# Sparse attention with two gated blocks on one core: PSUM as one pool of eight banks, two sets of scores at once, ScalarE subtracting half of the maxima, and the first y sums of both halves abreast

## The chip, the cores and the metric

The kernel runs on 1 core of one Trainium2 chip. The metric is device time in microseconds (us), the median of the runs of a kernel. The core has a matrix engine (TensorE, PE in the rows; its weight loads are PEld), a vector engine (VectorE, DVE), an activation engine (ScalarE, ACT), a general engine (GpSimd, POOL) and an engine that here only issues DMAs (SyncE, SP). Each engine executes its own instructions in the order in which they were written. Products are summed in PSUM, which has 8 banks of 512 fp32 columns over 128 partitions.

## The reference, cut to what matters

Three blocks follow each other, for a batch of 2, 768 positions, 8 heads of 64, and a width of 512:

```python
# attention: a window of 32 positions, and 24 summaries of 32 positions each
k_sum = k.reshape(B, H, nb, block, D).max(axis=3)
v_sum = v.reshape(B, H, nb, block, D).mean(axis=3)
scores_l = scale * np.matmul(q, k.transpose(0, 1, 3, 2))      # where |i-j| < 16
scores_s = scale * np.einsum('bhsd,bhnd->bhsn', q, k_sum) + np.log(block)
a = softmax(concatenate([scores_l_m, scores_s]));  x = a @ concatenate([v, v_sum])
# first block
theta = x @ w_theta
zr, zi = x * np.cos(theta), x * np.sin(theta)
y = np.einsum('ts,bsd->btd', w_tok_r, zr) + np.einsum('ts,bsd->btd', w_tok_i, zi)
u = x + y;  x = u + np.maximum(u @ w_ch, 0.0)
# second block
h = gelu(x @ w_in);  u, v = split(h);  v_n = layernorm(v) * g_ln
out = x + (u * (w_sg @ v_n + b_sg)) @ w_out
```

## The kernel before, in words

Every large product is made of three matmuls (`mm3`, L647 to L652: high by high, high by low, low by high), since each fp32 operand is split into a high and a low part by a copy and a subtraction.

The attention is cut into 8 pairs of heads (4 of each batch) and each pair into 2 halves of the sequence: 16 units, named by pair and half (`0_1` is pair 0, second half). A unit is a chain (`at_unit`, L871):

- `S`: PE lays masks (L881) and adds the scores (L890) in two PSUM banks, 3 tiles of 120 columns for each of 2 heads. That is one set of scores.
- `m`: DVE takes the 6 maxima (L923). `d`: DVE subtracts them (L929, 128x720) and writes `P` in SBUF; the set of scores is then free.
- `e`: ACT takes the exponential of `P` in place (L937, one instruction of 720 columns).
- `PT`, `Pt`: PE transposes `P` (L942, two groups of 3), ACT or DVE copies the result out of PSUM (L637, L642).
- `O`, `n`: PE multiplies by the values (L957, 24 matmuls), DVE divides by the sums (L967 to L971) and writes `x`.
- `X`, `xe`: PE transposes `x` (L980), ACT or DVE copies it to `xT`.

`ks` and `vs` are the summaries of k and v (L829, L837); `vp`, `vm`, `vr` lay the latter out with the values. Then `th` (L650 to L652 under `theta`) is x by w_theta, four groups of three matmuls of 512 columns for each of 12 tiles of 128 positions; `kk`, `rr`, `ab`, `sc`, `zm`, `zh`, `zl` turn it into sines and cosines times x, split into parts (`rotated`, L1036). `mixed` (L1072) sums y over the 6 tiles of a batch: 4 blocks of 6 matmuls (three of 512 columns into `y`, three of 256 into `ys`) for each tile and each half of the columns. A half of the columns needs 2 banks for `y` and 1 for `ys`. `uv` adds the result to `xT`. After that come `ch`, `iv`, `iu` (the products with w_ch and w_in), the layer norm, `Qp` (the product with w_sg, written to `Qs`) and `o` (the product with w_out, stored from SBUF).

The order of the work is made when the program is written. Each step is entered with `op` (L391): its engine or engines with an estimated duration, what it comes after, the buffers it takes and gives back, and a key. `Order.play` (L442) runs through these estimates and always takes the ready step with the smallest key. The keys come from three tables of numbers, `PLAN`, `LEAD` and `SHIFT`. Buffers have kinds: before, six single PSUM banks are of kind B and one pair of banks is of kind S, so that one set of scores exists at a time. Where the estimate has PE idle between 6 and 36 us, the planner puts in matmuls that nothing reads (`fill`, L707).

Of the kernel before, what the change touches and what calls it, by code (L numbers as in the profile page):

```python
# [8 lines left out]
F32 = mybir.dt.float32  # L9
# [6 lines left out]
ALU = mybir.AluOpType  # L16
# [21 lines left out]
    q_from=121.281, q_step=28.693, q_back=223.53, at0=-10.9, at0_pair=7.346, at0_half=2.395,  # L38
    at1=30.092, at1_pair=3.285, at1_half=4.867, th0=27.719, th0_step=4.256, th1=34.789,
    th1_gap=17.348, th1_step=24.005, y00=98.094, y00_step=24.656, y01=63.431, y01_step=19.591,  # L40
    y10=147.759, y10_step=8.224, y11=160.878, y11_step=12.492, k_early=56.892, vt_early=1.56,
    q_early=4.908, v_early=-11.766, s_early=11.963, pt=-73.034, o=3.795, x=51.425, y_gap=3,
    w_spare=2, v_spare=1, z_spare=6, y_spare=0, q_spare=2, table=13.626, mode=5.473, bsg=250.456,
    far0=6, far1=8, trees=109)
# [4 lines left out]
    Qz=74.168, ks=-40.136, vs=-11.881, vm=11.936, vr=-13.929, e=17.901, Pt=48.07, n=-10.669,  # L49
    xe=4.677, xh=9.148, xl=4.343, kk=-1.1, rr=-29.76, sc=-13.602, zm=-9.187, zh=7.556, zl=38.914,  # L50
    w_tht=8.728, w_rt=13.865, w_it=-1.048, w_rit=-8.999, k=-3.022, q=-3.059, v=1.199, vT=9.157,
    w_rd=22.528, w_id=-5.655, w_rid=3.014, w_thd=-9.579, bsg=-5.815, ch_e=13.7, d=14.634,
    gagf=-1.524, gh=8.649, gl=15.226, gm=-10.408, iu_g=88.574, iv_g=-16.768, m=-33.701,
    o_e=-19.883, rv=-3.588, sq=1.118, st=-55.633, tx=-19.318, tx_h=10.785, u=-3.396, u_h=-9.153,
    uv=-43.926, vh=6.864, vl=9.675, vo=-7.023, vp=0.039, w_chd=6.133, w_chh=-0.456, w_chl=3.459,
    w_chr=-13.975, w_cht=58.117, w_ih=-5.761, w_il=-46.919, w_inud=10.646, w_inuh=12.592,
    w_inul=-13.707, w_inur=8.343, w_inut=57.665, w_invd=15.806, w_invh=-50.158, w_invl=-21.398,
    w_invt=-8.855, w_ir=22.177, w_outd=-25.619, w_outh=15.605, w_outl=-21.45, w_outr=6.525,
    w_outt=12.079, w_rh=5.347, w_rih=6.258, w_ril=-15.3, w_rir=-13.172, w_rr=-12.082,
# [312 lines left out]
class Order:  # L372
# [69 lines left out]
    def play(self):  # L442
# [30 lines left out]
        while waiting:  # L473
# [36 lines left out]
            if e == "PE" and n > 1 and self.FILL_FROM < s < self.FILL_TO:  # L510
                out.append(self.filler(n, free_at["PE"], slots))
# [1088 lines left out]
```

## Time and profile before

| | |
|---|---|
| median of 3 runs | 382.21 us (379.33, 382.38, 382.21) |
| the profiled execution's own time | 380.85 us |
| its span, first to last instruction | 379.1 us |
| mean granted TensorE clock, share of full speed | 0.994 |
| PE busy | 369.4 us, 97% of the span, 2991 matmuls |
| DVE, ACT, POOL busy | 261.6, 204.1, 120.1 us |

In what follows a row of a view by line says: line, engine, operation, output<-inputs, shapes and how many, then busy us and the mean ns of one, then the idle time of the engine just before them and who ended it. A row of a timeline says: start us, length us, engine, line, operation, count, and in brackets the idle time of the engine before it with the releaser. A busy PE is not a PE at its peak, since the ends of matmuls are modelled: the distance from start to start tells its pace. PEclk is the granted TensorE clock, 1.00 being 2.4 GHz and 0.50 being 1.2 GHz.

### The profile page before, as it was taken

How to read it: one execution, taken by the hardware profiler on the slowest of the kernel's cores; microseconds unless marked ns; L12 is line 12 of the kernel's file. 1: busy time of each engine (PE TensorE's matmuls, PEld its weight loads, DVE VectorE, ACT ScalarE, POOL GpSimd, SP SyncE). 2: the span in 40 equal slices, each digit the busy share in tenths (PEclk: the TensorE clock that was granted, in tenths of full speed). 3: DMA queues.
4: the chain of work that ended last, by engine and by line, in shares of the span. 5: the costliest groups of instructions: out<-in, count | busy, mean ns of one | idle time of the engine just before them, and what ended most of it. 6: DMA issues, size and time to landing. Idle time of an engine off the chain costs nothing.

```text
span 379.1 us, 7679 instructions
## 1 busy us (share of the span) xinstructions
PE 369.4 (97%) x2991; PEld 321.9 (85%) x2991; DVE 261.6 (69%) x453; ACT 204.1 (54%) x349; POOL 120.1 (32%) x145
## 2 busy tenths in 40 slices
PE   8898999999999999999999999999999999999996
PEld 4786888888888888888888788888888999999996
DVE  4997999999975964436674968684134487689621
ACT  2586699967874862234743862458234876332100
POOL 6663488553310200002620163335000046521000
PEclk9998999999999999999999999999999999999999
DMA  7999897992005041002556921646021443511222
GB/s 267 334 338 305 297 315 191 316 345 70 0 9 215 2 145 62 2 0 80 182 171 240 355 99 64 228 158 218 0 83 43 125 144 106 158 52 58 91 103 84
DMA packets 27332, 57.38 MB, mean 151 GB/s; under 512 B 3424, under 2 KB 16800, under 8 KB 27296
## 3 DMA queue, kind: packets, MB, share of 16 engines
q1 hardware_dynamic: 27296, 56.90, 44.9%
q8 instruction: 23, 0.38, 0.4%
q14 instruction: 13, 0.11, 0.1%
HBM read 45.18 MB, written 11.40 MB: 149 GB/s over the span
## 4 chain that ended last, share of the span: by engine, by line
PE 82%; DMA 5%; DVE 5%; ACT 3%; issue 2%; POOL 1%; SPq 1%; POOLq 0%; DVEq 0%; ACTq 0%
PE y L650 6%; PE y L651 6%; PE y L652 6%; PE Qs L650 3%; PE Qs L651 3%; PE Qs L652 3%; PE ch L650 3%; PE ys L651 3%; PE ch L651 3%; PE ys L652 3%; PE iu L652 3%; PE iu L651 3%; PE ch L652 3%; PE iu L650 3%; PE iv L652 3%; PE iv L651 3%
## 5 line engine op out<-in xcount | busy, mean ns | idle before, releaser
L645 DVE TENSOR_TENSOR z<-f,z 128x512 fp32r<-128x512 f32 x21 | 14.9, 709 | 20.8 <-ACT z L637 20.6
L650 PE MATMUL Qs<-Qx,Qh 128*128 128x384 f32 x84 | 28.2, 336 | 0.2 <-DVE U L1458 0.2
L652 PE MATMUL Qs<-Qx,Ql 128*128 128x384 f32 x84 | 28.1, 334 | 0.0
L651 PE MATMUL Qs<-Qx,Qh 128*128 128x384 f32 x84 | 28.1, 334 | 0.0
L652 PE MATMUL ys<-w_ri,z 128*128 128x256 f32 x96 | 27.1, 282 | 0.0
L651 PE MATMUL ys<-w_ri,z 128*128 128x256 f32 x96 | 27.1, 282 | 0.0
L650 PE MATMUL ys<-w_ri,z 128*128 128x256 f32 x96 | 26.7, 278 | 0.0
L637 ACT ACTIVATE z<-f 128x512 fp32r<-128x512 f32 x19 | 11.9, 627 | 23.7 <-PE ys L652 18.1
L650 PEld LDWEIGHTS ys<-w_ri,z 128*128 128x128 f32 x96 | 18.0, 188 | 4.4
L637 ACT ACTIVATE Qx<-Qx 128x768 fp32r<-128x768 f32 x20 | 16.6, 843 | 9.3 <-DMA Qx<-dQx 6.4
L651 PEld LDWEIGHTS ys<-w_ri,z 128*128 128x128 f32 x96 | 18.0, 188 | 3.8
L650 PE MATMUL th<-w_th,xh 128*128 128x512 f32 x48 | 20.6, 428 | 0.2 <-DVE xT L642 0.2
L1061 DVE TENSOR_TENSOR f<-f,x 128x512 f32<-128x512 f32 x21 | 16.0, 763 | 5.4 <-ACT f L1055 5.1
L652 PE MATMUL th<-w_th,xh 128*128 128x512 f32 x48 | 19.3, 402 | 0.3 <-DVE xh L645 0.3
L650 PE MATMUL y<-w_i,z 128*128 128x512 f32 x48 | 19.3, 402 | 0.0
L651 PE MATMUL th<-w_th,xh 128*128 128x512 f32 x48 | 19.3, 401 | 0.0
L650 PE MATMUL y<-w_r,z 128*128 128x512 f32 x48 | 19.2, 399 | 0.0
L651 PE MATMUL y<-w_r,z 128*128 128x512 f32 x48 | 19.0, 397 | 0.0
L651 PE MATMUL y<-w_i,z 128*128 128x512 f32 x48 | 19.0, 395 | 0.0
L645 DVE TENSOR_TENSOR Ql<-vx,Qh 128x768 fp32r<-128x768 f32 x10 | 9.4, 960 | 13.7 <-PE iu L652 9.4
L650 PE MATMUL ch<-u,w_ch 128*128 128x512 f32 x48 | 18.8, 392 | 0.0
L650 PE MATMUL iu<-tx,w_inu 128*128 128x512 f32 x48 | 18.7, 390 | 0.0
(357 smaller groups left out, 1174.2 us busy)
## 6 DMA issues: line engine op xcount, KB each, us to landing
Qx<-dQx SPq DMA_DIRECT2D x21, 384.0 KB, 3.7
v<-in_vW_dram SPq DMA_DIRECT2D x16, 193.5 KB, 5.1
k<-in_kT_dram SPq DMA_DIRECT2D x8, 384.0 KB, 6.5
q<-in_qT_dram SPq DMA_DIRECT2D x16, 192.0 KB, 5.0
vT<-in_vT_dram SPq DMA_DIRECT2D x8, 384.0 KB, 5.2
w_r<-in_w_rT_dram SPq DMA_DIRECT2D x6, 511.8 KB, 5.0
w_i<-in_w_iT_dram SPq DMA_DIRECT2D x6, 511.8 KB, 5.6
Qw<-in_w_sgT_dram SPq DMA_DIRECT2D x12, 192.0 KB, 2.5
```

The lines of the kernel that those rows point to most:

```text
L637: ACT.activation(dst, src, AF.Copy, scale=scale)
L645: EN[e].tensor_tensor(out=lo, in0=src, in1=hi.bitcast(F32), op=ALU.subtract)
L650: PE.matmul(ps, ah, bh, start=first, stop=False, skip_group_check=True)
L651: PE.matmul(ps, ah, bl, start=False, stop=False, skip_group_check=True)
L652: PE.matmul(ps, al, bh, start=False, stop=last, skip_group_check=True)
L1061: EN[e].tensor_tensor(out=z3(), in0=z3(), in1=x.unsqueeze(1).to_broadcast([P, 2, 256]), op=ALU.mult)
```

## The change

Six things change; everything that is computed stays.

- **PSUM.** The eight banks become one tile, `banks`, cut into views of 512 columns, all of kind B. A set of scores takes an aligned pair of neighbouring free banks wherever there is one (`pairs`, `place`), so that two sets or more can be alive.
- **ScalarE subtracts.** For the second half of all 8 pairs (`lean` lists all eight) `d` goes. ACT makes minus an eighth of the 6 maxima (`mn`, 128x6), and takes the exponential straight from PSUM in 6 instructions of 120 columns, each with one column of these as its bias (`e..._0`, `e..._1`, three each). The set of scores is free after the last of them.
- **y abreast.** `mixed(0, (0, 1), ...)` sums both halves of the columns of batch 0 in one pass over the tiles: 4 banks for `y` and a pair for `ys`. Batch 1 is summed as before, one half after the other. The order in which z is made follows (`turn`).
- **Planner.** It now also reckons with the arrival of PE's instructions in blocks of 256 (`fetch`), and puts fillers between 5 and 60 us, from one matmul on.
- **Estimates.** Two durations are changed (`vo`, `Qn`).
- **Tables.** All numbers of `PLAN`, `LEAD` and `SHIFT` are new, so that nearly every step has another place.

```diff
 PLAN = dict(
-    q_from=121.281, q_step=28.693, q_back=223.53, at0=-10.9, at0_pair=7.346, at0_half=2.395,
+    lean=(1, 3, 5, 7, 0, 2, 4, 6), q_from=118.522, q_step=34.157, q_back=243.107, at0=-28.273,
+    at0_pair=-3.897, at0_half=4.51, at1=21.844, at1_pair=11.168, at1_half=-10.008, th0=52.144,
...
-    COUNT = {"W": 27, "H": 19, "X": 4, "K": 12, "V": 3, "Z": 3, "B": 6, "S": 1}
+    COUNT = {"W": 27, "H": 19, "X": 4, "K": 12, "V": 3, "Z": 3, "B": 8}
...
+    FETCH = 3.3
+    BLOCK, ASK, HAVE = 256, 246, 446
...
+        def pairs():
+
+            at = {int(b[1:]): x for x, b in slots["B"]}
+            return [(max(at[j], at[j + 1]), j) for j in range(0, 8, 2) if j in at and j + 1 in at]
...
-            made[name] = (ps_ if k in "BS" else cp).tile([P, n], dt, tag=order.where[name],
-                                                        name=name)
+            if k in "BS":
+                j = int(order.where[name][1:])
+                made[name] = banks[:, 512 * j:512 * j + SIZE[k]]
+                return made[name]
...
+        by_act = hf == 1 and p in PLAN["lean"]
+        if by_act:
+            def neg(e):
+                ACT.activation(T(f"m{u}")[:, 8:14], T(f"m{u}")[:, :6], AF.Copy, scale=-0.125)
+            op(f"mn{u}", {"ACT": 0.22}, neg, after=[f"m{u}"], use=[f"m{u}"])
+            for h in range(2):
+                def exps(e, h=h):
+                    for t in range(3):
+                        o = 360 * h + WC * t
+                        c = 512 * h + WC * t
+                        ACT.activation(T(f"P{u}")[:, o:o + WC], T(f"S{u}")[:, c:c + WC], AF.Exp,
+                                       bias=T(f"m{u}")[:, 8 + 3 * h + t:9 + 3 * h + t], scale=0.125)
+                op(f"e{u}_{h}", {"ACT": 0.67}, exps, after=[f"mn{u}"] + [f"e{u}_0"] * h, tab="exp",
+                   new=[] if h else [(f"P{u}", "W")], use=[f"S{u}", f"m{u}"] + [f"P{u}"] * h)
...
-    turn = [(b, h, i) for b in range(B) for h in range(2) for i in range(NT)]
+    turn = ([(0, h, i) for i in range(NT) for h in range(2)]
+            + [(1, h, i) for h in range(2) for i in range(NT)])
...
-    mixed(0, 0, PLAN["y00"], PLAN["y00_step"])
-    mixed(0, 1, PLAN["y01"], PLAN["y01_step"])
-    mixed(1, 0, PLAN["y10"], PLAN["y10_step"])
-    mixed(1, 1, PLAN["y11"], PLAN["y11_step"])
+    mixed(0, (0, 1), PLAN["y00"], PLAN["y00_step"])
+    mixed(1, (0,), PLAN["y10"], PLAN["y10_step"])
+    mixed(1, (1,), PLAN["y11"], PLAN["y11_step"])
```

The first place is PE's queue from the second set of scores on, in the kernel before (the digits behind a name are pair and half, the last number is the buffer's own; rows of masks are left out):

```order
L890 MATMUL S0_1_258<-k0_157,q0_1_169 64x96 x12
L890 MATMUL S0_1_258<-ks0_202,q0_1_169 64x24 x12
L846 MATMUL vp0_295<-ident_133,vs0_244 24x128
L942 MATMUL PT0_0_1_300<-ident_133,P0_0_252 120x128 x3
L942 MATMUL PT0_0_0_307<-ident_133,P0_0_252 120x128 x3
...
L890 MATMUL S1_0_322<-k1_173,q1_0_175 64x96 x12
L890 MATMUL S1_0_322<-ks1_254,q1_0_175 64x24 x12
L942 MATMUL PT0_1_0_356<-ident_133,P0_1_304 120x128 x3
```

The same place after (all of PSUM now has the name `banks`, so that the inputs tell which unit it is):

```order
L947 MATMUL banks_65<-k3_169,q3_0_171 64x96 x12
L947 MATMUL banks_65<-ks3_243,q3_0_171 64x24 x12
...
L947 MATMUL banks_65<-k2_173,q2_0_177 64x96 x12
L947 MATMUL banks_65<-ks2_279,q2_0_177 64x24 x12
...
L947 MATMUL banks_65<-k3_169,q3_1_202 64x96 x12
L947 MATMUL banks_65<-ks3_243,q3_1_202 64x24 x12
L1015 MATMUL banks_65<-ident_134,P3_0_325 120x128 x6
L1015 MATMUL banks_65<-ident_134,P0_0_245 120x128 x6
L903 MATMUL banks_65<-ident_134,vs3_315 24x128
```

Before, one set of scores follows the transposes of the set before it; after, four sets of scores (0_0, 3_0, 2_0 and 3_1) stand ahead of the first transpose.

The second place is ACT's queue at its first exponentials, before (`P` is the scores less their maxima, `Pt` the transposed ones, `xT` the transposed x):

```order
L937 ACTIVATE P0_0_252<-P0_0_252 128x720
L637 ACTIVATE ones0_187<-vp0_295 24x2x64
L637 ACTIVATE v0_0_199<-ones0_187 24x774
L937 ACTIVATE P0_1_304<-P0_1_304 128x720
L637 ACTIVATE Pt0_1_0_366<-PT0_1_0_356 120x384
L637 ACTIVATE ones1_189<-vp1_388 24x2x64
L937 ACTIVATE P1_0_386<-P1_0_386 128x720
```

And after (`m` holds the maxima, and behind them their negatives):

```order
L1010 ACTIVATE P2_0_362<-P2_0_362 128x720
L988 ACTIVATE m3_1_372<-m3_1_372 128x6
L694 ACTIVATE Pt0_0_1_418<-banks_65 120x384
L995 ACTIVATE P3_1_422<-banks_65,m3_1_372 128x120 x6
L694 ACTIVATE Pt2_0_1_447<-banks_65 120x384
L694 ACTIVATE Pt2_0_0_458<-banks_65 120x384
L694 ACTIVATE Pt3_1_0_474<-banks_65 120x384
L988 ACTIVATE m2_1_445<-m2_1_445 128x6
L995 ACTIVATE P2_1_508<-banks_65,m2_1_445 128x120 x6
```

For each second half, seven instructions stand where one of 720 columns stood.

The third place is DVE's queue at its start, before:

```order
L829 TENSOR_REDUCE ks0_202<-k0_157 128x24
L923 TENSOR_REDUCE m0_0_242<-S0_0_193 128x6
L929 TENSOR_TENSOR P0_0_252<-S0_0_193,m0_0_242 128x720
L829 TENSOR_REDUCE ks1_254<-k1_173 128x24
L923 TENSOR_REDUCE m0_1_290<-S0_1_258 128x6
L929 TENSOR_TENSOR P0_1_304<-S0_1_258,m0_1_290 128x720
```

And after:

```order
L886 TENSOR_REDUCE ks0_200<-k0_158 128x24
L980 TENSOR_REDUCE m0_0_239<-banks_65 128x6
L886 TENSOR_REDUCE ks3_243<-k3_169 128x24
L1002 TENSOR_TENSOR P0_0_245<-banks_65,m0_0_239 128x720
L886 TENSOR_REDUCE ks2_279<-k2_173 128x24
L980 TENSOR_REDUCE m3_0_285<-banks_65 128x6
L1002 TENSOR_TENSOR P3_0_325<-banks_65,m3_0_285 128x720
L980 TENSOR_REDUCE m2_0_357<-banks_65 128x6
```

Three k summaries are now made ahead of the maxima of the second set, and no subtraction follows for the second halves. In the whole queue of PE the attention of batch 0 and of the first pairs of batch 1 now stands ahead of the first `th`: 13 units' scores, where it was 8 before.

## Rows read from the trace of the kernel before

**Rows 1.** The page, part 1: busy time, share of the span, instructions.
```profile
PE 369.4 (97%) x2991; PEld 321.9 (85%) x2991; DVE 261.6 (69%) x453; ACT 204.1 (54%) x349; POOL 120.1 (32%) x145
```

**Rows 2.** By stretch: length, busy PE, PEld, DVE, ACT, POOL, PEclk, DMA share, GB/s.
```profile
9.00:36.00 27.00, 22.92 (x549) 19.89 (x542) 24.38 (x46) 18.81 (x36) 15.89 (x25) 0.95 1.02 331
36.00:72.00 36.00, 35.59 (x612) 29.37 (x611) 33.16 (x59) 31.70 (x51) 23.47 (x29) 0.99 0.86 272
72.00:100.00 28.00, 27.56 (x294) 23.22 (x293) 26.62 (x48) 21.41 (x38) 12.37 (x12) 1.00 0.53 188
100.00:300.00 200.00, 200.00 (x1008) 170.11 (x1007) 122.86 (x204) 103.90 (x186) 43.41 (x44) 1.00 0.34 115
300.00:376.00 76.00, 75.64 (x444) 75.15 (x442) 50.45 (x96) 25.90 (x40) 18.99 (x16) 1.00 0.29 101
```

**Rows 3.** Waits of PE in the whole span: total us, times, longest.
```profile
PE S L881 <- DVE P L929: 1.3, 4, 0.4
```

**Rows 4.** Timeline of PE from 21 to 33 us.
```profile
21.91 0.92 PE L957 MATMUL O<-v,Pt 120*64 120x65 f32 x24
22.76 0.32 PE L881 MATMUL S<-maskb,identb 64*64 64x288 bf16 x4
...
23.81 0.87 PE L942 MATMUL PT<-ident,P 128*120 128x128 f32 x6
24.52 0.27 PE L846 MATMUL vp<-ident,vs 128*24 128x128 f32 x1
24.63 0.82 PE L980 MATMUL X<-ident,x 128*128 128x128 f32 x6
25.38 1.10 PE L957 MATMUL O<-v,Pt 120*64 120x65 f32 x24
...
30.25 0.50 PE L890 MATMUL S<-k,q 64*64 64x96 f32 x14
32.46 0.41 PE L890 MATMUL S<-k,q 64*64 64x96 f32 x9 [1.72 <-issue]
```

**Rows 5.** By stretch, around the gap in rows 4; columns as in rows 2.
```profile
30.00:34.00 4.00, 2.28 (x63) 1.99 (x60) 2.81 (x5) 2.28 (x4) 2.56 (x2) 0.93 1.02 327
34.00:38.00 4.00, 4.00 (x35) 3.18 (x34) 2.44 (x6) 2.75 (x6) 0.00 (x0) 0.65 0.87 285
```

**Rows 6.** The page, part 3: a queue, its packets, MB, share of 16 engines.
```profile
q8 instruction: 23, 0.38, 0.4%
```

**Rows 7.** Timeline of DVE at its start.
```profile
6.33 0.91 DVE L923 TENSOR_REDUCE m<-S 128x6 f32<-128x720 f32 x1 [1.71 <-PE S L890]
7.28 0.91 DVE L929 TENSOR_TENSOR P<-S,m 128x720 f32<-128x720 f32 x1
8.10 0.94 DVE L829 TENSOR_REDUCE ks<-k 128x24 f32<-128x768 f32 x1
```

**Rows 8.** Group of PE's fillers, by line and shape.
```profile
L710 PE MATMUL fill_B<-maskb,identb 128*128 128x480 bf16 x9 | 2.0, 367 | 0.0
```

**Rows 9.** Groups of ACT's instructions by line and shape, up to 110 us.
```profile
L937 ACT ACTIVATE P<-P 128x720 f32<-128x720 f32 x16 | 12.8, 803 | 6.4 <-DVE P L929 6.2
L637 ACT ACTIVATE Pt<-PT 120x384 f32<-120x384 f32 x24 | 10.7, 486 | 5.5 <-PE PT L942 5.2
L1054 ACT ACT_TABLE_LOAD x4 | 5.1, 1283 | 0.1
L937 ACT ACT_TABLE_LOAD x3 | 3.8, 1283 | 0.1
L1054 ACT ACTIVATE f<-f,half_pi 128x256 f32<-128x256 f32 x6 | 3.0, 507 | 0.1
L1055 ACT ACTIVATE f<-rr 128x256 f32<-128x256 f32 x6 | 2.4, 402 | 0.0
L637 ACT ACTIVATE ones<-vp 24x128 f32<-24x128 f32 x3 | 0.8, 268 | 2.6 <-PE vp L846 2.6
```

**Rows 10.** Timeline of ACT, two copies of transposes in one row.
```profile
16.49 0.87 ACT L637 ACTIVATE Pt<-PT 120x384 f32<-120x384 f32 x2 [0.85 <-PE PT L942]
```

More of the change, by code (lines that the diff above doesn't have):

```diff
@@ L440, in filler, with fetch @@
         return o
+    def fetch(self, n, d, s):
+        late, at, end = 0.0, self.at, self.at + n
+        while True:
+            ask = self.ASK + self.BLOCK * len(self.come)
+            have = self.HAVE + self.BLOCK * self.had
+            if ask <= have:
+                if ask >= end:
+                    break
+                t = s + late + max(0, ask - at) * d / n
+                self.come.append(max(t, self.come[-1] if self.come else 0.0) + self.FETCH)
+            else:
+                if have >= end:
+                    break
+                t = s + late + max(0, have - at) * d / n
+                late += max(0.0, self.come[self.had] - t)
+                self.had += 1
+        self.at = end
+        return late
     def play(self):
         self.link()
+        self.at, self.had, self.come = 0, 0, []
         free_at = {"PE": 1.3, "DVE": 0.85, "ACT": 0.7, "POOL": 0.7, "SP": 0.7}
@@ L513, in play @@
             f = s + o.eng[e]
+            if e == "PE":
+                if n > 0 and self.FILL_FROM < s < self.FILL_TO:
+                    self.fetch(2 * n, n * self.FILL, free_at["PE"])
+                code = "".join(c for c in o.name if not c.isdigit()).strip("_")
+                f += self.fetch(self.CODE.get(code, 24), o.eng[e], s)
             free_at[e] = f - self.OVER[e]
@@ L527, in play @@
             for b, k in o.new:
[L528 to L530 removed]
+                self.where[b] = place(k, s)
             for b in o.use:
@@ L1102, in mixed @@
-        last[0] = pre
-        for j in range(2):
-            d = 2 * h + j
-            for half, (o, w) in enumerate(HALVES):
-                def ev(e, d=d, j=j, half=half, o=o, w=w):
-                    ps = T(f"y{b}_{d}")[:] if half == 0 else T(f"ys{b}_{h}")[:, sl(j, 256)]
-                    dst = xT[:, d, b * S + o:b * S + o + w]
-                    DVE.tensor_tensor(out=dst, in0=ps, in1=dst, op=ALU.add)
-                op(f"uv{b}_{d}_{half}", {"DVE": dve(w)}, ev, after=pre,
-                   use=[f"y{b}_{d}" if half == 0 else f"ys{b}_{h}"])
+                ys, c0 = rest(h, j)
@@ new lines, in mixed, with ev @@
+                for half, (o, w) in enumerate(HALVES):
+                    def ev(e, d=d, half=half, o=o, w=w, ys=ys, c0=c0):
+                        ps = T(f"y{b}_{d}")[:] if half == 0 else T(ys)[:, c0:c0 + 256]
+                        dst = xT[:, d, b * S + o:b * S + o + w]
+                        DVE.tensor_tensor(out=dst, in0=ps, in1=dst, op=ALU.add)
+                    op(f"uv{b}_{d}_{half}", {"DVE": dve(w)}, ev,
+                       after=[f"y{b}_{NT - 1}_{2 * h + 1}_1"],
+                       use=[f"y{b}_{d}" if half == 0 else ys])
@@ L1220, in norm @@
                                       op1=ALU.mult)
-            op(f"vo{b}_{i}", {"ACT": act(512), "DVE": 0.54}, norm, after=[f"rv{b}"], use=[vx],
+            op(f"vo{b}_{i}", {"ACT": 0.8, "DVE": 0.54}, norm, after=[f"rv{b}"], use=[vx],
                port=("DVE",))
```

750 lines of the change are left out of this document (387 added, 363 removed).

## The prediction

> **What bounds the kernel now.** I read the busy times first: PE is busy 97% of the span [rows 1]. Then I cut the span into stretches, since an average over stages hides where the rest lies. From 100 to 300 us PE is never idle, from 300 to 376 it misses 0.36 us, from 36 to 72 it misses 0.41 and from 72 to 100 it misses 0.44 us. Between 9 and 36 us it misses 4.08 us of 27 [rows 2]. So PE bounds everything, and only the attention at the start leaves room. Together this is 5.29 us of idle PE.
>
> Who ends these waits? Four times, 1.3 us in all, the masks of a new set of scores wait until DVE has subtracted the maxima of the set before, since there is one set [rows 3]. The largest wait is another: in the middle of a set, at 30.75 us, PE stands for 1.72 us, and the releaser is "issue", so that no semaphore was missing [rows 4]. I take this for a late supply of instructions. A queue of 23 packets carries 0.38 MB of them [rows 6], and that is some 64 bytes for each of PE's 2 x 2991 instructions [rows 1]; at that moment the data DMAs use their whole share, 1.02 [rows 5]. Behind the gap the granted clock is a mean of 0.93 in one stretch of 4 us and of 0.65 in the next, which is a part of each at the lower level of 1.2 GHz [rows 5]. Against full clock that loses 4 x 0.07 + 4 x 0.35 = 1.7 us. The sum of idle and slow time is 7.0 us.
>
> The profiled execution took 380.85 us, its span of 379.1 and 1.75 around it. That lies between the runs (379.33 to 382.38) and 0.4% under their median of 382.21. My sum is against 380.85. PE's matmuls are the same before and after but for one more filler, and one filler is 2.0 / 9 = 0.22 us [rows 8]. So no order can bring more than 7.0 us: 373.9 is the floor.
>
> **The change part by part.** *Two sets of scores.* The 1.3 us of rows 3 go. What is late next is the first chain. In the new order DVE makes, from the first maxima at 6.33 us on, a k summary, a subtraction, another k summary, then the maxima of set 3_0 and their subtraction. The distance from one to the next is 0.82 us for such an instruction (7.28 to 8.10 [rows 7]), so the subtraction ends at about 6.33 + 5 x 0.83 + 0.91 = 11.4, the exponential (0.80 [rows 9]) at 12.3, and the first transpose can start at 12.4. Until then PE has three sets at 1.05 us (22.76 to 23.81 [rows 4]) and ten fillers (2.2), from 6.3 to 11.6. It waits about 0.9 us. That is a new wait, once.
>
> *ScalarE subtracts half.* DVE loses 8 subtractions, 8 x 0.82 = 6.6 us; it was busy 24.38 of 27 us in the early stretch [rows 2], so this is relief on an engine that PE waits for. ACT loses 8 exponentials of 720 columns (0.80 each) and gets 8 times one instruction of 6 columns and six of 120 with a bias column. No row shows one of 120 columns from PSUM with a bias. From below: the 384-column copy takes 0.486 and the 720-column one 0.803, or 0.94 ns a column, so 120 columns would be 0.24, and since two copies of 0.486 end in 0.87 [rows 10], the next starts 0.10 before the end of the last: 0.14 each. From above: the 256-column sine with a bias, 0.507 less 0.10 is 0.41. I take the nearest row: 24x128 from PSUM, 0.268, plus what the bias costs, 0.507 against 0.402 on one shape, 0.105 [rows 9], less 0.10: 0.27.
>
> Does ACT hold PE up? I count both queues to the transposes of unit 5_0, where ACT is closest. ACT starts at 9.0 (the subtraction of unit 0_0, now behind one k summary). Ahead of the transposes stand 14 copies of transposes and 12 other copies of 384 columns (26 x 0.39 = 10.1), 6 long exponentials (6 x 0.70 = 4.2), 36 short ones (36 x 0.27 = 9.7), 6 of 6 columns (0.2 each, 1.2), and 11 others: 6 spreads of the summaries over 774 columns and a weight copy, priced like the long exponential (4.9), and 4 short copies (0.8). The sum is 30.9, so that ACT is there at 39.9 at the earliest. PE starts its transposes at 12.4 and has 22 groups of transposes (0.355 each, 7.8), 8 sets (8.4), 11 times O (0.85, 9.4), 8 times X (0.375, 3.0) and 6 vp (0.7) [rows 4]: it is there at 41.7. ACT is ahead by 1.8 us. It stays ahead up to 0.27 + 1.8 / 36 = 0.32 us for a short exponential; at 0.41 it comes at 44.9 and PE loses 3.2 us, at 0.14 nothing. I take 1.0 us for the small waits of this stretch, since ACT never had so little slack before.
>
> The Trainium skill speaks against this part: the page "ScalarE: Activation LUTs", section "What ACT_TABLE_LOAD costs", gives an activation with a bias column about 93 ns more than one without, 280 + 0.833 ns a column, with an overlap of about 93 ns. The trace agrees on the first, 105 ns by rows 9. By the page a short exponential would come every 0.29 us, an estimate, ACT would be at the transposes of unit 5_0 0.7 us later, and the sum would not change.
>
> ACT also saves table loads: 7 changes between exponential and sine in the rows (4 and 3, 1.28 us each [rows 9]), 3 in the new order, 5.1 us. They lay beside PE's work on `th`, and I count them as cover for the y stage and not as time.
>
> *Instruction supply.* PE's queue is denser now: attention first, no `th` between. From 12.4 to 41.7 us it holds 8 sets of 52 matmuls, 264 for O, 66 transposes, 30 more, 776 in 29 us or 26 a us; between 9 and 36 us it was 549 in 27, 20 a us [rows 2]. The planner now spaces them by a rule for blocks of 256, but nobody has seen the rule hold. From below: no wait. From above: two such gaps with a slow clock once, 2 x 1.72 + 1.7 = 5.1. One gap with its slow clock (3.4) is what 27 us of the sparser order brought. I take 1.2, nearer to none, because some gaps will fall where PE waits for `P` anyway.
>
> *y of both halves abreast.* Same matmuls, same number. It takes 4 banks and a pair, and leaves 2 for `th`; the order has y blocks between one `th` and the next, and their release lies beside them. A tile of 8 blocks lasts PE as long as two tiles of one half did. From 72 to 100 us, where this starts, ACT was busy 21.4 of 28 and DVE 26.6 [rows 2]; DVE is ahead by its 6.6 us. From 36 us on PE missed 0.41 + 0.44 + 0.36 = 1.2 us; I take 1.1. From above, a wait of 0.6 for each of the six `th` of batch 1 would be 3.6; from below all of the 1.2 goes.
>
> *One tile for PSUM, new estimates.* No cost. If the one tile made false waits, sets would again come one after the other; in the new order the set 3_1 stands behind set 2_0 with nothing of DVE between.
>
> The sum: 380.85 - 7.0 + 0.2 (a filler) + 0.9 + 1.0 + 1.2 + 1.1 = 378.25, say 378.2. This is 0.7% below the profiled execution and 1.05% below the median.
>
> **The rivals.** *The supply never binds.* If PE never stands for instructions, 1.2 us fall away: 377.0. For it: rows 4 show one such gap, and from 100 to 300 us there is none [rows 2]. Against it: the gap fell in the stretch which is now denser. The Trainium skill's page "Runtime: NRT & Kernel Launch", section "Instruction fetch mechanics", would have it so: instructions come in blocks of 256 ahead of time, and the cost is mostly hidden. The 1.72 us of rows 4 are not hidden, so I trust it by half.
>
> *It binds more.* Two gaps and a slow clock, 5.1 in place of 1.2: 382.1. For it speaks the density, against it that a gap needs saturated DMA queues too, and that PE's own waits give the supply time.
>
> *ScalarE becomes the bound, slower than before.* If a short exponential comes every 0.41 us, ACT's queue ends 3.2 us behind PE at unit 5_0. These waits come in pieces over six units, and the clock would fall as it did behind the gap of rows 4; twice 1.7 us. 378.2 + 3.2 + 3.4 = 384.8, and 381.4 if the clock holds. It decides at 0.32 us. Against it: 24 partitions by 128 columns took 0.268 alone.
>
> *The change does not do what it says* (false waits on the one tile): the old waits stay and ACT has more to do, 383 or more. The order speaks against it.
>
> **How the numbers follow.** Forecast 0.46, supply never binds 0.25, supply binds more 0.15, ScalarE 0.12, false waits 0.02. What a measurement here can tell from no change is about 1%, or 377.0 counted from the profiled execution and 378.4 from the median. The forecast lies at that edge, so half of it is faster (0.23), with most of the first rival (0.21): 0.44. Slower by over 1% is most of the ScalarE case and of the false waits: 0.10. The rest, 0.46, is within 1%. The range goes from 374.5, near the floor, to 383.0, which leaves out the worst of the ScalarE case.
>
> **What would show it.** Right: no wait of the masks for the subtraction of the set before; the first transposes near 12.4 us; a short exponential every 0.25 to 0.30 us; ACT over 95% busy from 12 to 40 us; PE idle between 9 and 45 us of 2 to 3 us; from 100 us on no idle PE, as before. Wrong: "issue" gaps of over 1.5 us in all, a granted clock under 1.00 in more than one stretch, PE waits for `P` from ACT of over 2 us in all, or waits of y or `th` beyond 80 us of over 1.5 us.

## The result, and the profile after

The change made the kernel slower by a little: a median of 382.93 us over 20 runs (378.98 to 387.72) against 380.15 us over 20 runs of the kernel before on the same chips. The ratio is 1.0059, with a 95% interval of 1.0039 to 1.0079; the two slow runs of the changed kernel, 386.33 and 387.72 us, are left out of it. The forecast was 378.2 us. The profiled execution of the changed kernel took 383.47 us, its span 381.7, against 380.85 and 379.1 before. Each kernel has a trace of one execution, so that the single waits below are those of that execution.

The page, part 1, answers to [rows 1], and PE has one matmul more, as forecast:

```profile
PE 367.7 (96%) x2992; PEld 322.2 (84%) x2992; DVE 254.9 (67%) x425; ACT 208.3 (55%) x403; POOL 131.1 (34%) x151
```

Busy PE is 1.7 us less than before and the span 2.6 us longer, so PE stood idle for 4.3 us more. The same five stretches as in [rows 2] (length, busy PE, PEld, DVE, ACT, POOL, PEclk, DMA share, GB/s) show where:

```profile
9.00:36.00 27.00, 21.13 (x536) 19.02 (x535) 20.16 (x41) 17.68 (x49) 14.76 (x26) 0.94 0.85 269
36.00:72.00 36.00, 32.50 (x674) 28.09 (x674) 31.66 (x57) 30.13 (x72) 13.18 (x16) 1.00 0.87 271
72.00:100.00 28.00, 27.63 (x205) 23.05 (x205) 25.10 (x45) 23.63 (x46) 8.58 (x9) 1.00 0.71 245
100.00:300.00 200.00, 200.00 (x1005) 169.88 (x1004) 122.02 (x191) 108.03 (x196) 67.50 (x61) 1.00 0.33 112
300.00:376.00 76.00, 75.93 (x441) 75.46 (x440) 50.89 (x87) 26.87 (x42) 23.01 (x22) 1.00 0.32 108
```

PE misses 5.87 us of the first stretch (4.08 before) and 3.50 of the second (0.41 before), and next to nothing later. The waits of PE over the whole span say for what (total us, times, longest):

```profile
PE banks L947 <- issue: 4.5, 2, 2.6
PE banks L1030 <- issue: 3.3, 2, 2.1
PE banks L1030 <- DMA w_th<-in_w_theta_dram: 1.6, 1, 1.6
PE banks L760 <- DVE warm L747: 1.3, 1, 1.3
PE banks L1015 <- ACT P L1010: 0.4, 1, 0.4
```

The masks no longer wait for a subtraction: [rows 3] has no successor. ScalarE costs PE 0.4 us, once. What is left is "issue", 7.8 us in four stops, where [rows 4] had one of 1.72, and one of 1.6 us put down to the load of `w_th`. The timeline of PE has the five (start, duration, engine, line, what, count, idle time before it and its releaser):

```profile
10.84 0.48 PE L947 MATMUL banks<-ks,q 64*64 64x24 f32 x22
13.93 0.29 PE L947 MATMUL banks<-ks,q 64*64 64x24 f32 x2 [2.61 <-issue]
...
22.25 1.32 PE L1030 MATMUL banks<-v,Pt 120*64 120x65 f32 x37
24.78 0.57 PE L1030 MATMUL banks<-v,Pt 120*64 120x65 f32 x11 [1.21 <-issue]
...
29.31 0.85 PE L1030 MATMUL banks<-v,Pt 120*64 120x65 f32 x21
32.22 2.74 PE L1030 MATMUL banks<-v,Pt 120*64 120x65 f32 x51 [2.05 <-issue]
...
42.57 0.37 PE L947 MATMUL banks<-ks,q 64*64 64x24 f32 x16
44.81 0.31 PE L947 MATMUL banks<-ks,q 64*64 64x24 f32 x8 [1.87 <-issue]
...
52.01 0.92 PE L1030 MATMUL banks<-v,Pt 120*64 120x65 f32 x24 [1.63 <-DMA w_th<-in_w_theta_dram]
```

The first four cut the 24 equal matmuls of a unit in two, as the narrow scores at 10.84 and 13.93 (22 and 2); there the inputs are those of the matmuls just done. The fifth stands before matmuls that read `v` and `Pt` and not `w_th`, so they did not need the load that the view names. That this stop is one of the five shows when the matmuls between the stops are counted. These are windows cut at the stops, with the columns as above:

```profile
0.00:13.90 13.90, 10.06 (x222) 6.12 (x222) 8.16 (x10) 3.25 (x4) 6.56 (x23) 1.00 0.88 297
13.90:24.70 10.80, 9.64 (x251) 8.65 (x252) 9.48 (x17) 9.70 (x29) 7.11 (x13) 1.00 0.81 243
24.70:32.20 7.50, 5.39 (x125) 4.76 (x125) 3.95 (x10) 4.78 (x12) 4.14 (x6) 1.00 0.88 279
32.20:44.70 12.50, 10.72 (x251) 9.88 (x251) 9.89 (x20) 10.17 (x29) 6.89 (x10) 0.86 0.73 238
44.70:52.00 7.30, 5.58 (x127) 4.76 (x127) 6.76 (x12) 6.59 (x16) 2.99 (x4) 1.00 0.99 335
```

222 matmuls come before the first stop, and then 251, 125, 251 and 127: once or twice some 126 matmuls, each with its weight load. That is once or twice 252 instructions, and 256 of the 64 bytes that the prediction worked out are one packet of 16 KB; the few that are missing I take for PE's semaphore instructions, which the rows do not list. The kernel before had 596 ahead of its only stop, about 222 + 3 x 125. So PE stops where a packet of instructions ends and the next has not come. In the trace the packet's own record ends 1.3 to 1.6 us before PE goes on, at all five stops. (In the texts written before the runs these places are called 97 + 128n; that counts PE's semaphore instructions as matmuls.)

Counted so, the supply cost 2.61 + 1.21 + 2.05 + 1.87 + 1.63 = 9.37 us, which is all of the idle PE from 9 to 72 us (5.87 + 3.50), and a slow clock behind the third stop. All of the idle PE between 9 and 376 us is 9.8 us (5.29 before). Only 0.4 us of it, at 73.8 us, is a wait for another engine: of that the old order had 3.6.

### The profile page after: what moved, and what is told of

Read it like the earlier page. It is cut to its first block, busy times and chain, and to the rows that moved or that the text cites. A ratio compares the mean times of both kernels' runs of the same rounds, so it can differ in the third digit from the quotient of the medians.

```text
span 381.7 us, 7729 instructions
## 1 busy us (share of the span) xinstructions
PE 367.7 (96%) x2992; PEld 322.2 (84%) x2992; DVE 254.9 (67%) x425; ACT 208.3 (55%) x403; POOL 131.1 (34%) x151
## 3 DMA queue, kind: packets, MB, share of 16 engines
HBM read 45.18 MB, written 11.40 MB: 148 GB/s over the span
## 4 chain that ended last, share of the span: by engine, by line
PE 87%; DVE 4%; DMA 3%; issue 3%; ACT 1%; SPq 1%; POOL 0%; POOLq 0%; DVEq 0%; ACTq 0%
PE banks L707 25%; PE banks L708 25%; PE banks L709 24%; PE banks L1030 3%; PE banks L947 3%; PE banks L1015 3%; DMA w_th<-in_w_theta_dram 2%; PE banks L1053 2%; DMA out_dram<-o_1s 1%; PE banks L938 1%; DVE gx L702 1%; PE banks L760 1%; PE banks L767 1%; POOL U L1470 0%; DVE g L702 0%
## 5 line engine op out<-in xcount | busy, mean ns | idle before, releaser
L709 PE MATMUL banks<-Qx,Ql 128*128 128x384 f32 x84 | 28.1, 334 | 0.0
L708 PE MATMUL banks<-Qx,Qh 128*128 128x384 f32 x84 | 28.1, 334 | 0.0
L707 PE MATMUL banks<-Qx,Qh 128*128 128x384 f32 x84 | 28.1, 334 | 0.0
L709 PE MATMUL banks<-w_ri,z 128*128 128x256 f32 x96 | 27.1, 283 | 0.0
L708 PE MATMUL banks<-w_ri,z 128*128 128x256 f32 x96 | 27.1, 282 | 0.0
L707 PE MATMUL banks<-w_ri,z 128*128 128x256 f32 x96 | 26.7, 278 | 0.0
L1273 DVE BATCH_NORM_STATS2 st<-vx 128x6 f32<-128x512 f32 x12 | 8.2, 681 | 21.0 <-ACT vx L1263 21.0
L707 PEld LDWEIGHTS banks<-w_ri,z 128*128 128x128 f32 x96 | 18.0, 188 | 4.4
L708 PEld LDWEIGHTS banks<-w_ri,z 128*128 128x128 f32 x96 | 18.0, 188 | 3.8
L1030 PE MATMUL banks<-v,Pt 120*64 120x65 f32 x384 | 15.4, 233 | 4.9 <-issue 3.3
L707 PE MATMUL banks<-w_th,xh 128*128 128x512 f32 x48 | 19.7, 410 | 0.0
L707 PE MATMUL banks<-w_r,z 128*128 128x512 f32 x48 | 19.2, 401 | 0.0
L1030 PEld LDWEIGHTS banks<-v,Pt 120*64 120x64 f32 x384 | 13.5, 145 | 6.6 <-issue 4.5
L707 PE MATMUL banks<-w_i,z 128*128 128x512 f32 x48 | 19.1, 397 | 0.0
L708 PE MATMUL banks<-w_i,z 128*128 128x512 f32 x48 | 19.0, 396 | 0.0
L708 PE MATMUL banks<-w_r,z 128*128 128x512 f32 x48 | 19.0, 396 | 0.0
L708 PE MATMUL banks<-w_th,xh 128*128 128x512 f32 x48 | 18.8, 392 | 0.0
L709 PE MATMUL banks<-w_th,xh 128*128 128x512 f32 x48 | 18.8, 391 | 0.0
```

The source lines that it names most:

```text
L707: PE.matmul(ps, ah, bh, start=first, stop=False, skip_group_check=True)
L708: PE.matmul(ps, ah, bl, start=False, stop=False, skip_group_check=True)
L709: PE.matmul(ps, al, bh, start=False, stop=last, skip_group_check=True)
L1030: PE.matmul(ps[64 * ab:64 * ab + 64, o:o + 65], sb[:WC, t * P + 64 * ab:t * P + 64 * ab + 64], v[:WC, c:c + 65], start=True, stop=True)
L1273: DVE.bn_stats(out=st, in_=vf())
```

## The experiments

**Theory A** was: PE gets its instructions in blocks of 256 (128 matmuls with their loads), one after the other, and the denser order asks for them faster than they come. **Theory B**: the stops belong to the work at those places, which needs something that comes late and that the profile does not name. **Theory C**: ScalarE, which now subtracts, is the bound, and the stops cover for it.

**1. Shift the blocks.** The warm-up matmuls (512 columns) and the fillers (480) are cut into four, so that 48 more matmuls stand ahead of most of the scores.

```diff
-PE.matmul(ps[:], warm[:, :P], warm[:, P:640], start=True, stop=True)
+for x in range(4):
+    PE.matmul(ps[:, sl(x)], warm[:, :P], warm[:, P + 128 * x:256 + 128 * x], start=True, stop=True)
...
```

> The changed kernel with the same work in the same order, but each warm-up and filler matmul cut into four of a quarter of the columns, so that 48 more matmuls (each with its weight load) stand ahead of the scores that follow them. In the changed kernel PE stops without a semaphore ahead of matmul number 225 (counted from 1 as issued, it stops when 224 to 225 are done), 481, 609, 865 and 993: all of the form 97 + 128n. Theory A (instruction supply: PE gets its instructions in blocks of 256, 128 matmuls with their weight loads, and stops where a block has not come): the waits stay at these counts, so they move to work that stands 48 matmuls earlier in the program: the first from the last narrow scores of S3_1 to its first masks or wide scores, the second from values O2_0 to scores S1_1, the third from O0_0 to S0_1, the fourth from S5_0 to S5_1, the fifth from O5_1 to O4_1; 4 to 6 waits, 6 to 11 us in all, time within 1% of the changed kernel. Theory B (the stop belongs to the work at that place: something it needs comes late that the profile does not name): the waits stay at the same units of work, at counts 48 higher, with the same lengths.

Measured: 379.2 us, ratio to before 0.9989 (0.9958 to 1.0021). Windows cut at the stops, as above:

```profile
0.00:11.90 11.90, 9.44 (x222) 8.33 (x222) 6.92 (x9) 2.90 (x4) 5.32 (x20) 1.00 0.83 274
11.90:17.70 5.80, 5.09 (x126) 4.70 (x127) 5.03 (x8) 4.18 (x14) 3.10 (x6) 1.00 1.05 330
17.70:37.20 19.50, 19.04 (x502) 16.82 (x501) 17.07 (x39) 17.89 (x50) 13.75 (x23) 1.00 0.90 287
37.20:43.20 6.00, 5.06 (x126) 4.06 (x127) 5.39 (x9) 5.94 (x19) 4.97 (x6) 1.00 1.00 337
```

222 again, then 126, 502 (four times 125.5), 126. The stops come after 222, 348, 850, 976 and 1,102 matmuls; in the changed kernel they came after 222, 473, 598, 849 and 976. Three counts stayed, the other stops lie on the same steps of 125.5, and the work at them is other work. The first stop now cuts the masks of set 3_1, as expected, where the changed kernel stopped in that set's last scores. Theory B falls. The second stop has another name in the view, `Pt` from ACT:

```profile
18.05 0.27 PE L1018 MATMUL banks<-ident,P 128*120 128x128 f32 x1 [0.72 <-ACT Pt L694]
```

I count it with the others since it stands at such a step and a packet ends 1.4 us before it. The length was a miss: 1.5, 0.7, 0.4, 0.6 and 0.9 us, 4.2 in place of 6 to 11, and the clock did not fall in these windows (1.00). So the time fell by some 0.7%, and I do not know how much of that is where the limits lie and how much is when the packets met the data loads.

**2. Fewer instructions, same order.** The two window parities of a block share the keys of the narrow scores, so that one matmul with 128 queries can take the place of two with 64.

```diff
-PE.matmul(s[64 * ab:64 * ab + 64, c:c + WK] if wide else
-          s[64 * ab:64 * ab + 64, c + WK:c + WC],
...
+elif not ab:
+    PE.matmul(s[:, c + WK:c + WC], q[rr, 128 * t:128 * t + 128],
+              T(f"ks{p}")[rr, :NS],
+              start=False, stop=True, skip_group_check=True)
```

> The changed kernel in the same order, but the narrow scores (24 columns) of the two window parities of a block, which share their keys, are one matmul of 128 queries instead of two of 64: 24 matmul records fewer per... exactly 12 fewer matmuls of the profile and 12 fewer weight loads in each of 16 units, the result the same. Theory A (supply): 384 of some 2,000 instructions of the attention go, so fewer blocks fall due in the dense stretch and the path from a block's request to its limit holds more work; waits without a semaphore fall from 9.4 us (five, the one put down to the w_th load among them) to 3 to 6 us, the time by 3 to 6 us, to 377 to 380 us, level with or below the kernel before. Theory B (late data or releases at those places): the waits stay at 8 to 10 us and the time changes by the matmul time alone, within 1 us. Theory C (ScalarE is the bound and the stops only cover for it): the time stays within 1 us and PE's waits for P from ACT grow by what the others lose.

Measured: 379.14 us, ratio 0.9993 (0.9964 to 1.0021). All waits of PE in this run, and its groups of scores (count, busy, mean ns):

```profile
PE banks L760 <- DVE warm L747: 1.3, 1, 1.3
PE banks L1018 <- ACT P L1013: 0.4, 1, 0.4
```

```profile
L953 PE MATMUL banks<-ks,q 64*128 64x24 f32 x192 | 13.7, 271 | 0.0
L948 PE MATMUL banks<-k,q 64*64 64x96 f32 x384 | 11.2, 251 | 0.0
```

And the last of the first four sets, with the transposes behind it, in the timeline:

```profile
12.56 0.85 PE L953 MATMUL banks<-ks,q 64*128 64x24 f32 x12
13.34 1.52 PE L1018 MATMUL banks<-ident,P 128*120 128x128 f32 x12
```

Every stop is gone, where 3 to 6 us were expected to stay, and the "load of `w_th`" with them; nothing took their place. That is against theories B and C. What was not expected is the price: a set's narrow scores last 0.85 us where they lasted 0.48, and a whole set, masks and scores, takes some 0.44 us longer. Sixteen times 0.44 is 7.0 us of PE's time for the 9.4 of the stops.

**3. The same merge in the kernel before.**

> The kernel before, with the same merge of the narrow scores. Theory A (supply): its one wait of 1.72 us and the waits that were just covered become shorter, so the time falls by 0.5 to 2 us, less than the changed kernel gains. Theory B and C: no change beyond 0.5 us, and the wait stays at 1.7 us.

Measured: 383.5 us, ratio 1.0116 (1.0072 to 1.016). Its one stop went too, but the expectation missed the price: plus 7.0 for sixteen merged sets, less 1.72 for the stop and 1.7 for the slow clock behind it [rows 4, 5], is plus 3.6 us; 4.0 were measured. Together with the last run: the same edit brings the changed kernel 2.5 us and costs the kernel before 4, because the first stands still 9.4 us for want of instructions and the second 1.72.

**4. ScalarE's half undone, the order kept.** In the eight units DVE subtracts again and one exponential of 720 columns follows, at the places in the queues where ScalarE's short ones stood.

```diff
-for t in range(3):
-    ...
-    ACT.activation(T(f"P{u}")[:, o:o + WC], T(f"S{u}")[:, c:c + WC], AF.Exp,
-                   bias=T(f"m{u}")[:, 8 + 3 * h + t:9 + 3 * h + t], scale=0.125)
+if h == 0:
+    sub(e)
+    x = T(f"P{u}")[:, :720]
+    ACT.activation(x, x, AF.Exp, scale=0.125)
```

> The changed kernel in its own order and with its banks, but ScalarE's half of the subtractions undone: in the eight units of the second half DVE subtracts and ScalarE takes one exponential of 720 columns again (at the places in the queues where the short ones stood). DVE gets 8 x 0.82 us, ScalarE loses 8 x (6 x 0.27 + 0.2 - 0.8) = 8 us. Theory A (supply sets the dense stretch): the waits without a semaphore get shorter by what PE now waits for DVE, and the time changes by less than 2 us either way. Theory C (the ScalarE path costs the time): the time falls by 2 us or more. If the split is what removed the waits for the subtraction and nothing else hides them, the time rises by 3 to 7 us, with new waits of PE on P from ACT or on DVE.

Measured: 384.29 us, ratio 1.0105 (1.006 to 1.015), 0.5% over the changed kernel, with intervals that overlap. PE waits 2.9 us for `P` from ACT, four times, and 0.9 for loads of `q`; the stops for instructions, after 222, 474, 600 and 852 matmuls, shrink to 4.8 us. What one wait gave up (4.6 us) the others took for the most part (3.8), as theory A has it; part of it is also that the first packet starts at 10.04 us here and at 11.40 in the changed kernel. Theory C wanted 2 us or more of gain, so it falls; giving ScalarE half of the subtractions costs nothing that this run shows.

**5. The supply by itself.** A stream of 1,152 small matmuls (64x64 tile, 24 columns) that wait for nothing, and then 1,152 more beside 39 loads of 384 KB; nothing of the reference is computed.

> Nothing of the reference is computed (the output is zeros): PE runs 1,152 small matmuls of one 64x64 tile and 24 columns (bf16 zeros) that wait for nothing, first with no data transfer under way, then, after the first of 40 loads of 384 KB has landed, 1,152 more beside the other 39 loads. Theory A (instruction supply): in both parts PE stops without a semaphore every 128 matmuls; a block takes in the quiet part about what the quiet stages of the two traces show from PE's passing instruction 128 of a block to the use of the next but one (2.2 us to the start of its packet, 1.0 us for the packet, 1.4 us after it: 4.6 us), and beside the loads 5.5 to 8 us, 1.2 to 1.7 times as much. Theory A without the loads' part (the supply is slow by itself, not because of the loads): the same period in both parts. Theory B (the stops belong to places in the program): a steady stream without waits, 15 to 40 ns a matmul in both parts.

The timeline of PE, the quiet part and then the loaded one:

```profile
1.24 3.17 PE L82 MATMUL banks<-warm 64*64 64x24 bf16 x223 [1.24 <-DVE warm L74]
5.74 1.89 PE L82 MATMUL banks<-warm 64*64 64x24 bf16 x128 [1.33 <-issue]
9.19 1.89 PE L82 MATMUL banks<-warm 64*64 64x24 bf16 x128 [1.57 <-issue]
12.92 1.89 PE L82 MATMUL banks<-warm 64*64 64x24 bf16 x128 [1.84 <-issue]
...
42.79 1.89 PE L82 MATMUL banks<-warm 64*64 64x24 bf16 x128 [4.14 <-issue]
48.99 1.89 PE L82 MATMUL banks<-warm 64*64 64x24 bf16 x128 [4.31 <-issue]
55.18 1.89 PE L82 MATMUL banks<-warm 64*64 64x24 bf16 x128 [4.31 <-issue]
...
73.77 1.89 PE L82 MATMUL banks<-warm 64*64 64x24 bf16 x128 [4.31 <-issue]
77.22 1.89 PE L82 MATMUL banks<-warm 64*64 64x24 bf16 x128 [1.56 <-issue]
```

223 matmuls, then exactly 128 between two stops. From one start to the next it is 3.45 to 3.73 us without loads (9.19 - 5.74, 12.92 - 9.19) and 6.20 us beside them (48.99 - 42.79), at a DMA share of 1.03 and 402 GB/s. When the loads are done it is 3.45 us again (77.22 - 73.77). So in this stream the supply is 128 / 3.6 = 36 matmuls a us at rest and 128 / 6.2 = 20.6 beside full data queues. The quiet period is shorter than the 4.6 us that I expected.

**6. More instructions in the kernel before.** Each wide score matmul (96 columns) is cut into two of 48.

> The kernel before in its own order, but each wide score matmul (96 columns) is cut into two of 48: 24 more matmul records and 24 more weight loads in each of 16 units, the same columns and result. Theory A (supply): before's order is spared only because its dense stretch asks for instructions just slowly enough; with 768 more instructions in it the one wait of 1.7 us becomes 4 to 6 waits, 5 to 10 us in all, all at matmul counts 97 + 128n, and the time rises by those and by the matmuls' own 16 x 0.1 to 0.45 us: 1.5 to 4 per cent. Theory B: the wait stays the one of 1.7 us, at the same unit of work, and the time rises by the matmuls' own part alone, at most 2 per cent.

Measured: 386.98 us, ratio 1.0179 (1.0125 to 1.0233). Three stops, 0.95, 2.29 and 0.72 us, 4.0 in all, where four to six of 5 to 10 us were expected; the one before was 1.72. The first two come after 348 and 599 matmuls, on the steps of 125.5 again and at other work. PE's busy time rose by 4.4 us (373.8 against 369.4), most of the loss. The stops moved and grew as theory A has it, but the time alone does not decide, since theory B allowed up to 2% too. The first stretch:

```profile
9.00:36.00 27.00, 22.00 (x691) 19.35 (x690) 21.39 (x39) 16.29 (x30) 13.83 (x24) 1.00 0.90 297
```

That is 691 matmuls in 27 us, 25.6 a us, where the same order had 549 [rows 2].

**7. Tell the planner.** The planner assumed a block to be asked for after 246 instructions of the one before and usable 3.3 us later. For this run it was told 128 and 5.6, and its table of shifts was searched anew against that.

```diff
-FETCH = 3.3
-BLOCK, ASK, HAVE = 256, 246, 446
+FETCH = 5.6
+BLOCK, ASK, HAVE = 256, 128, 446
```

> The changed kernel with the same operations, but its planner is told the supply as the traces show it: a block asked for when 128 records of the one before it are done (it assumed 246), usable 5.6 us after that and after the block before it (it assumed 3.3), 446 records as the limit kept; the table of shifts was searched anew against that, so the order of the attention stretch differs. Told the measured supply, the planner counts 9 us of stops in the changed kernel's own order, as the trace has 9.4, and some 4 in this one. Theory A (supply): 3 to 6 us of stops without a semaphore, all at matmul counts 97 + 128n, time 1 to 4 us under the changed kernel: 0.995 to 1.003 of the kernel before. Theory B (the stops belong to the operations): 7 to 10 us of stops remain, time within 1 us of the changed kernel (1.003 to 1.009).

Measured: 382.71 us, ratio 1.0059 (1.0039 to 1.0079): no gain, a miss. The profiled execution took 732.66 us, nearly twice the median, for a reason that stays open, so the stops are read from another execution of the same kernel:

> The replanned kernel again, for a profile of an undisturbed execution; its time is known, level with the changed kernel. Theory A: 4 to 9 us of stops without a semaphore at counts 97 + 128n, that is, the search moved them but did not remove them, since a block takes 5 to 8 us where the planner counts 5.6. Otherwise (stops under 3 us) the order that the search found waits for something else: 3 us or more of waits for DVE, ScalarE or a load that the changed kernel does not have.

382.43 us; two stops of 4.2 us in all, and 2.2 us of small waits for ACT, DVE and a load, which the changed kernel does not have. The stops went down as expected and the time did not follow; the small waits and a busy PE of 2.1 us more (369.8 against 367.7) took it back. Of these 2.1 us the planner's own fillers are 1.0: the new order has twelve (3.4 us), the changed kernel ten (2.4). Where the rest comes from stays open.

**8. Replanned with eleven units merged.**

> As the replanned kernel, with the narrow scores merged (one matmul of 128 queries for two of 64) in eleven of the sixteen units, 1_0, 1_1, 2_0, 2_1, 3_0, 3_1, 4_0, 4_1, 5_0, 5_1 and 6_1, at 0.44 us of PE time each (as the merged kernel's trace shows), and an order searched for that. Theory A (supply): no stops without a semaphore above 1 us in all; of 9.4 us 4.8 are paid for the merged matmuls, so the time is 3 to 5 us under the changed kernel: 0.992 to 0.999 of the kernel before. Theory B: as the all-merged kernel or worse, 0.999 or above.

Measured: 378.98 us, ratio 0.9963 (0.9944 to 0.9982). No stop for instructions at all, as expected, and the first version that beats both kernels.

**9. Pay only where PE would stand.** The shifted kernel of experiment 1, in the changed kernel's order, with the merge in three units alone, and then in four.

```diff
+    ... merge=("3_1", "4_0", "5_0"),           # then ("3_1", "1_0", "4_0", "5_0")
```

> The shifted kernel (warm-up and filler matmuls cut into four), with the narrow scores merged in three units alone, S3_1, S4_0 and S5_0, which stand between the request and the limit of the blocks that came late there. Theory A (supply): 36 matmuls fewer, three times 0.44 us of PE time that mostly falls into time in which PE would stand still; the stops without a semaphore shrink from 4.2 to 1.5 to 3.5 us, and the time by 0 to 2 us against the shifted kernel: 0.994 to 0.999 of the kernel before. Theory B: the stops stay and the time rises by 1.3 us, to 1.002.

> The shifted kernel with three merged units, plus a fourth, S1_0, which stands between the request and the limit of the block that still came 1.5 us late there (at matmul 481, in the values O3_1). Theory A (supply): 0.44 us of PE time falls into the stop, which shrinks to 0.4 to 0.9 us; the time falls by 0.3 to 0.6 us, 0.988 to 0.992 of the kernel before, unless the 12 matmuls fewer bring another block's limit into a dense place. Theory B: the stop stays at 1.5 us and the time rises by 0.4 us.

Measured: 376.57 us, ratio 0.991 (0.9883 to 0.9938), and 375.72 us, ratio 0.9876 (0.984 to 0.9911): the best version of this study. Both are a little better than expected (0.994 to 0.999, then 0.988 to 0.992). With three merged units a stop of 1.47 us is left after 474 matmuls, with four it is gone. The second one's waits of PE, and its first two stretches:

```profile
PE banks L761 <- DVE warm L747: 1.3, 1, 1.3
PE banks L951 <- issue: 0.4, 1, 0.4
PE banks L1023 <- ACT P L1018: 0.4, 1, 0.4
PE banks L941 <- issue: 0.3, 1, 0.3
```

```profile
9.00:36.00 27.00, 26.68 (x685) 23.65 (x677) 24.71 (x50) 22.89 (x62) 17.63 (x29) 1.00 0.98 300
36.00:72.00 36.00, 35.21 (x609) 29.77 (x602) 33.31 (x63) 31.10 (x73) 15.32 (x19) 1.00 0.94 315
```

685 matmuls in the first 27 us, 25.4 a us, where the changed kernel had 536 and the kernel before 549 [rows 2]. Its span is 7.9 us under the changed kernel's: 8.7 us of stops and 1.7 of slow clock there less, four merged units (1.8) more, 8.6 by this count.

**10. Does the shift help any order?**

> The kernel before, with its warm-up and filler matmuls cut into four as in the shifted kernel (45 matmuls more ahead of the attention). Theory A (supply): its blocks fall due at other places; it has one stop of 1.7 us and three limits met with nothing to spare, so the stops come to 0 to 4 us, at counts 97 + 128n, and the time is 0.995 to 1.008 of the kernel before; the gain of the shifted kernel is thus no gain that cutting the fillers gives any order. If cutting the fillers gains by itself (an earlier start of the scores, say), the time is 0.993 or less here too.

Measured: 380.98 us, ratio 1.0009 (0.9979 to 1.004). One stop of 1.43 us, after 597 matmuls (596 before), now in a transpose of the results and no longer in the scores. So cutting the fillers gives nothing by itself. Whether a few merged units would help the kernel before as well was not tried. An upper bound, estimated: without this stop and the 1.7 us that the slow clock behind such a stop cost in [rows 5] it would take 380.98 - 1.43 - 1.7 = 377.9 us, still over the 375.72 of the changed order.

## Why the prediction was wrong

By its own steps:

- *Which stage, and what kind of wait.* Right. PE bounds, the early attention is the only place with room, and the 1.72 us of rows 4 was a late supply of instructions. Of the 3.6 us that PE was idle before, beside that stop, 0.4 is left.
- *Two sets of scores* (-1.3). Right; the masks wait for no subtraction. The new wait, 0.9 us before the first transposes at 12.4 us, is there and costs nothing by itself. The exponential that the first transposes read ends at 11.34 + 0.80 = 12.14 us, near the 12.3 of the prediction, but the first stop (2.61, from 11.32 to 13.93) lies over it, and they start at 14.15. In experiments 2 and 9 PE comes from the scores, longer by the merge, at 13.34 and 13.17 and starts them without a wait. The row of the timeline of ACT:

```profile
11.34 0.80 ACT L1010 ACTIVATE P<-P 128x720 f32<-128x720 f32 x1 [1.81 <-DVE P L1002]
```

- *ScalarE* (+1.0). Too much. A short exponential was taken at 0.27 us; six of them in 1.61 us with 0.366 for one make (1.61 - 0.366) / 5 = 0.25. PE waited 0.4 us for `P`, at 73.8 us, and between 9 and 72 us never for ACT; short waits may lie under the stops. ACT was not over 95% busy but 72% (20.16 of 28 us from 12 to 40); in the last kernel of experiment 9, where the stops are nearly gone, it was 91% (25.61). The Trainium skill's page "ScalarE: Activation LUTs", section "What ACT_TABLE_LOAD costs", gave an estimate of 0.29, so the trace is a little below it. The row of the timeline of ACT, and that of its groups from 9 to 72 us:

```profile
16.28 1.61 ACT L995 ACTIVATE P<-banks,m 128x120 f32<-128x120 f32 x6
```

```profile
L995 ACT ACTIVATE P<-banks,m 128x120 f32<-128x120 f32 x42 | 11.8, 366 | 2.2 <-DMA k<-in_kT_dram 2.0
```

- *y abreast and later waits* (+1.1). Too much: from 72 to 376 us PE misses 0.44 us, the wait for `P` among them, and no wait of y or `th` is named.
- *Instruction supply* (+1.2). **This is the step that failed.** The stops measured 9.4 us, and the slow clock behind the third cost 1.7, an estimate from 12.5 us at 0.86 in place of 1.00: 11.1 in all, far over the upper bound of 5.1. Between 9 and 45 us PE was idle for 7.7 us, where 2 to 3 had been forecast. The bound was made by counting gaps: one was seen, so two at most. But one visible gap did not mean that gaps are rare. In the trace of the kernel before, the packets due at some 347, 473 and 596 matmuls end 1.4, 1.4 and 1.3 us before PE goes on there, the same distance as at the stops. So three packets in a row came with nothing to spare, of which the last alone shows as a long stop, and the prediction's own 26 matmuls a us against 20 asked for them sooner.

How much sooner is too soon is known only in part. At the 20.6 matmuls a us of experiment 5 the 776 matmuls from 12.4 to 41.7 us need 37.7 us and were given 29.3: 8.4 us too few, against 9.4 measured over a stretch of 43 us. That this comes so near is in part luck, for the supply has no fixed rate: beside DMA shares of 0.90 and 0.98, experiment 6 got 25.6 matmuls a us and the last kernel of experiment 9 got 25.4. Its packets start at 9.20, 14.47, 19.41, 23.99 and 29.40 us, those of the changed kernel at 11.40, 16.95, 22.37, 29.77 and 34.50. Why they come later and further apart in the changed kernel stays open; the data loads are a candidate, since the stream shows that they can delay packets.

By the rival "it binds more" the mechanism was on the list, at 0.15 and 382.1 us, and this is what came, with five stops where it had two. That its time fits, and that 382.93 lies within the range up to 383.0, is luck. With 11.1 in place of 1.2 the sum gives 388.1 us against the 383.47 of the profiled execution. Of the 4.7 us between them 4.5 are found, in terms that came out smaller: the first chain by 0.9, ScalarE and the later waits by 1.7 (0.4 of 2.1), and PE's busy time by 1.9. The sum has 369.4 - 1.7 + 0.2 = 367.9 us for it without slow clock; 367.7 were measured with 1.7 of slow clock in them. So "PE's matmuls are the same", on which the floor of 373.9 rests, does not hold to 2 us; why is open. The argument against that rival, that a gap needs saturated DMA queues, is wrong: the quiet part of experiment 5 stops 1.3 to 1.8 us at every block at a DMA share of 0.02.

The rule weighed in the first rival, from the Trainium skill's page "Runtime: NRT & Kernel Launch", section "Instruction fetch mechanics", that blocks of 256 come ahead and are mostly hidden, holds here for the blocks and from 100 us on for the hiding; in the dense stretch the trace disagrees, with 1.2 to 2.6 us not hidden at each of five blocks, and the measurement decides.

That nothing else held the change back is shown by experiment 9: the changed order with the supply nearly out of the way runs at 375.72 us, under the forecast of 378.2, even with 1.8 us paid for merged scores, and the shift alone gives the kernel before nothing (experiment 10). The change removed the waits that it was made for; the denser order then met a supply that was already at its limit.

## What to carry to other kernels

Where "issue" stands before a group of small matmuls that is cut in two, count the matmuls from one such stop to the next; if it is the same number each time, or a multiple of it, instructions are the likely limit, whatever releaser the row names. Then do not count the gaps seen so far: look in the trace how long before its use each packet of the instruction queue lands. Where several come with nothing to spare, an order that asks for instructions faster is likely to stop there. Here fewer and larger matmuls in that stretch eased it (experiments 2, 8 and 9). They pay best where PE would stand anyway: by the ratios, four merged units brought the shifted kernel 4.3 us, all sixteen brought the changed kernel 2.5.

## What the runs showed of the hardware

- In the stream PE goes on with the next 128 matmuls every 3.45 to 3.73 us without data loads and every 6.20 us beside them, 1.7 times as long, though a packet of 16 KB itself takes about 1 us in the trace in either case. In the kernels, beside loads, the supply reached 25.4 and 25.6 matmuls a us over 27 us (experiments 9 and 6).
- A releaser can be a bystander: 1.63 us were put down to a load that the waiting matmuls do not read, and vanished with the other stops (experiment 2).
- Behind the third stop of the changed kernel the clock is at its lower level for a part of the next 4 us (a mean of 0.61, row below), as behind the one stop before [rows 5]. In the first two stretches of experiments 1, 2, 8 and 9 it is 1.00. But not every stop brings it down: it is 1.00 behind the first stop of the changed kernel, the longest with 2.61 us, and behind the 2.29 us of experiment 6.

```profile
32.00:36.00 4.00, 3.79 (x56) 3.65 (x56) 2.74 (x9) 1.87 (x7) 1.25 (x4) 0.61 0.65 234
```

- One matmul for 128 queries in place of two for 64 on quarters of the array halves the instructions and takes longer: 0.85 us a set against 0.48.
